# Reordered loads, a longer lead for the gate products and finer routing pieces in a fused attention and mixture-of-experts kernel

## Chip, cores, metric

One core of one Trainium2 chip runs the whole kernel in one launch. All arithmetic is in f32. The metric is the time of one execution on the device in microseconds (us), here the median of 3 runs. Engines are called by the profile's names: PE is TensorE, DVE VectorE, ACT ScalarE, POOL GpSimd, SP SyncE.

## What is computed

The input is q, k, v of 8 batches, 8 heads, 576 positions and 64 channels, and the weights of 8 experts. First comes causal attention in which a position sees itself and the 63 before it; then a mixture of experts on the rows x (4608 rows of 512) that attention gives:

```
scores = where((rel >= 0) & (rel < 64), q @ k.T / sqrt(64), -1e9)
x      = (softmax(scores) @ v), heads side by side          # [8, 576, 512]
logits = x @ w_gate                                          # 8 experts
local  = sigmoid(x @ w_local)
e      = argmax(logits) where s == 0 or local < 0.5, else the e of s - 1
out    = softmax(logits)[e] * (relu(x @ w1[e]) @ w2[e])      # w1 512x1024, w2 1024x512
```

So each row goes to one expert, and whether a row takes its own choice or that of the row before it is settled by a scan along the sequence.

## The kernel before, in words

**Attention** works through 9 superchunks (`sc`) of 512 rows, and in each through 4 pairs of heads (`hp`): 36 units. A unit is `scores` (36 matmuls at L325 into a score bank; ACT's exp at L341; DVE's multiply by a mask at L344) and `values` (32 matmuls at L354; then DVE's reciprocal L359 and products L362 and L364, which make `x`). Scores run two units ahead of values (`LEAD`). Between them PE does helper work, described below.

The orders of PE, ACT and SP are those in which the program is written (`manual_schedule`). POOL and DVE are ordered by a scheduler, which lets DVE run routing work ahead. So where an instruction stands in the text is where it stands in PE's, ACT's and SP's queue, and an early wait there holds up all that is written later.

**Loads.** SP issues them. k and q of a superchunk are four transfers of 512 KB (L198, L199), one pair of heads' halves each, into a ring of four 2 MB slots, which later takes the expert weights too. `va` (L193) holds v with a column of ones behind each head. `vb` holds the same values moved by half a chunk of 128 rows; `shift` fills it by copies, ACT's at L301, L304 and L308, POOL's at L302 and L306 (`shift_first` for superchunk 0, L315 to L317). It is a generator: one or two of its copies are issued per unit, from hp 1 of the superchunk before. `load(sc + 2)` is written at hp 0 and 2 of superchunk sc. `until` (L205) is a transfer of 4 bytes, whose only use is that SP has to wait for what it reads: the loads of superchunk 1 come behind the first mask, those of superchunk 2 behind the reciprocal of unit (0,2).

**Gate.** The logits of x are needed for routing, and they are made in one of two ways. For superchunks 0 to 3, x is transposed by PE (`turn`, L249, copied to SBUF at L252), multiplied with the gate weights (`gates`, L261 to L265; ACT copies the result `gs` at L268), transposed back (`back`, L273), and summed over heads by DVE (`logits`, L279). For superchunks 4 to 8 (from `TURNED` on) the product is taken with v itself, ahead of attention: a transposed v, `vtt`, is loaded (L188), `gates` multiplies it, `back` transposes the result back, and `spread` copies it into 9 further columns of va and vb (ACT L290, L291 and once L293 into vb, DVE L294 into va). `values` then has 74 columns instead of 65, and its weighted sum gives the logits' share of each head along with x. `gates(sc + 1)` is written at hp 2 and `spread(sc + 1)` at hp 3 of superchunk sc.

**PSUM.** Two score banks, and two more tiles of two banks' width, `ps_x`, which values, turn, gates and the routing pieces share. `ps_x` is one pool of two buffers.

**Routing.** `Router.first` routes the first 14 chunks of 128 rows (the first three sequences): argmax, the scan that carries the last fresh choice on (L728 to L758), ranks within an expert, and tables of row numbers (`idx1`, by matmuls at L874). It is a generator too. Each `yield` gives a weight, an estimate of the DVE time since the last one; `step()`, called twice per unit, takes the next piece once the weights, reduced by `HALF` = 0.8 per call, are used up:

```python
    def step():
        nonlocal pause, side
        pause -= HALF
        if side and pause <= 0.0:
            w, trip = next(side, (0.0, None))
            pause = max(pause, -HALF) + w
            if trip is None:
                side = ()
                if ex.jobs:
                    ex.rows(ex.jobs[0], -1)
```

The generator starts at unit (4,2). When it ends, and if the weights of the first expert job have been asked for, the last lines issue the gather of that job's rows (`ex.rows`, POOL L1023, tile `xg`). x of each superchunk is written to DRAM by POOL at L449 (`xs`, 1 MB); gathers read it from there, and both use the same software queue.

**Experts.** `Experts.run` takes six first jobs of 128 rows (numbered from −1), during which `Router.second` routes what remains, and then larger ones of 256 rows. A job gathers its rows, transposes them (PE L1048 into `tp`, copied to `xt` at L1049), multiplies by w1 (`hp`, L1190 and L1099), and by w2 (L1221, L1142), and scatters its rows to the output (POOL L1172). Weights come through the ring (L1035).

Of the kernel before, what the change touches and what calls it, by code (L numbers as in the profile page):

```python
# [60 lines left out]
TURNED = 4  # L61
# [86 lines left out]
def attention(ctx, tc, ring, q, k, v3, v4, vt, xs, lt, ok, wg, wg2, ident, rt, ex):  # L148
# [12 lines left out]

    nc = tc.nc
    cp = ctx.enter_context(tc.tile_pool(name="at_const", bufs=1))
# [4 lines left out]
    ps_x = ctx.enter_context(tc.tile_pool(name="at_ps_x", bufs=2, space=PSUM))  # L168
# [4 lines left out]
    def width(sc):  # L173
        return VX if sc < TURNED else VW

# [3 lines left out]
    def load(sc, parts):  # L179
        t = slice(sc * SC, (sc + 1) * SC)  # L180
        src = v3[t] if sc < TURNED else v4[t.start - TURNED * SC:t.stop - TURNED * SC]
        for part in parts:
            if part == "turned":
                vtt = vts[sc] = kp.tile([P, HP, WIN + SC], F32, name="vtt", bufs=1)

                a = 0 if sc == TURNED else WIN
                at = (sc - TURNED) * SC + a
                nc.sync.dma_start(out=vtt[:, :, a:], in_=vt[:, :, at:at + WIN + SC - a])  # L188
            elif isinstance(part, tuple):
                if sc not in vas:  # L190
                    vas[sc] = space("va", sc)
                h = slice(*part)
                nc.sync.dma_start(out=vas[sc][:, :, h], in_=src[:, h].rearrange("(c p) h x -> p c h x", p=P))  # L193
            else:
                if sc not in kts:
                    both = ring.tile([P, 2, HP, SC], F32, name="w")
                    kts[sc], qts[sc] = both[:, 0], both[:, 1]
                nc.sync.dma_start(out=kts[sc][:, part], in_=k[:, part, t])  # L198
                nc.sync.dma_start(out=qts[sc][:, part], in_=q[:, part, t])  # L199
# [11 lines left out]
    def warm(n):  # L211

        r = ps_x.tile([P, 2, SC], F32, name="xo")
        for _ in range(n):
            nc.tensor.transpose(r[:, 0, :P], ident, ident)

    warm(20)
# [13 lines left out]
    for i in range(2):  # L231
        m = cp.tile([P, KB, 2, WIN], F32, name=f"mask{i}")
        for c in range(2):
            h = slice(c * WIN, (c + 1) * WIN)
            for par in range(2):
                nc.vector.tensor_scalar(m[h, :, par, :], colf[h], rowf[h], None, Alu.is_ge if par == c else Alu.is_lt)
        mid = MID[i]
        other = slice((1 - mid % 2) * WIN, (2 - mid % 2) * WIN)
        nc.vector.memset(m[other, mid // 2, mid % 2, :], 0.0)
        masks.append(m.rearrange("p a b q -> p (a b q)"))  # L240

    allr = cp.tile([P, NSC, HP, 2, 4], F32, name="allr")

    def turn(sc, x, half):

        r = ps_x.tile([P, 2, SC], F32, name="xo")
        for i in range(2):
            for c in range(4):
                nc.tensor.transpose(r[:, i, c * P:(c + 1) * P],  # L249
                                    x[:, c, 2 * half + i].rearrange("p j d -> p (j d)"), ident)  # L250
        o = pp.tile([P, 2, SC], F32, name="p")
        nc.scalar.copy(o, r)  # L252
        vts.setdefault(sc, []).append(o)

    def gates(sc):

        r = ps_x.tile([P, 2, SC], F32, name="xo")
        for hp in range(HP):
            h = slice(hp * GW, (hp + 1) * GW)
            if sc < TURNED:  # L260
                nc.tensor.matmul(r[h, 0, :], lhsT=wg[:, hp, :], rhs=vts[sc][hp // 2][:, hp % 2], start=True, stop=True)  # L261
                continue
            nc.tensor.matmul(r[h, 0, :], lhsT=wg2[:, hp, :], rhs=vts[sc][:, hp, WIN:], start=True, stop=True)
            if sc == TURNED:
                nc.tensor.matmul(r[h, 1, :WIN], lhsT=wg2[:, hp, :], rhs=vts[sc][:, hp, :WIN], start=True, stop=True)  # L265
        n = SC + WIN if sc == TURNED else SC
        gs = wk.tile([P, SC + WIN], F32, name="gs", bufs=1)
        nc.scalar.copy(gs[:, :n], r.rearrange("p i x -> p (i x)")[:, :n])  # L268
        return r, gs
# [11 lines left out]
    def spread(sc, gated):  # L281

        r, gs = gated
        by_head = back(r, gs).rearrange("p (c h g) -> p c h g", c=4, h=H)
        gt = by_head[:, :, :, :E + 1]
        g = slice(VX, VW)
        if sc == TURNED:
            o = r[:WIN, 0, :P]
            nc.tensor.transpose(o, gs[:, SC:], ident)
        nc.scalar.copy(vbs[sc][:WIN, :, :, g], gt[:WIN])  # L290
        nc.scalar.copy(vbs[sc][WIN:, 1:, :, g], gt[WIN:, :3])  # L291
        if sc == TURNED:
            nc.scalar.copy(vbs[sc][WIN:, 0, :, g], o.rearrange("p (h g) -> p h g", h=H)[:, :, :E + 1])  # L293
        nc.vector.tensor_copy(vas[sc][:, :, :, g], gt)  # L294
# [24 lines left out]
    def scores(sc, hp):  # L319
# [24 lines left out]
        nc.vector.tensor_tensor(p, p, m.to_broadcast([P, 2, SC]), op=Alu.mult)  # L344
        return p

    def values(sc, hp, p, x, g):
        va, vb, n = vas[sc], vbs[sc], width(sc)
        xo = ps_x.tile([P, 2, SC], F32, name="xo")
# [11 lines left out]
        if sc >= TURNED:  # L361
            nc.vector.tensor_tensor(g[:, :, hp].rearrange("p c j e -> p j c e"), o[:, :, :, VX:],  # L362
                                    rr.to_broadcast([P, 2, 4, E + 1]), op=Alu.mult)
# [4 lines left out]
    ps = {}  # L368
    for u in units[:LEAD]:
        ps[u] = scores(*u)  # L370
        warm(16)
    shift_first(0)
    until(0, masks[0][:1, :1])
# [16 lines left out]
    def psum():  # L390
        return ps_x.tile([P, 2, SC], F32, name="xo")[:, 0, :]

    for i, (sc, hp) in enumerate(units):
        if hp == 0:
            x, g = wk.tile([P, 4, HP, 2, DH], F32, name="x"), None
            if sc >= TURNED:
# [4 lines left out]
        if hp == 1 and sc + 1 < NSC:  # L401
            moves = shift(sc + 1)
        for _ in range(2):
            next(moves, None) if moves else None
        if hp == HP - 1:
            if sc + 1 < NSC and sc + 1 >= TURNED:
                spread(sc + 1, gated)
            if sc < TURNED:
                turn(sc, x, 0)
                old = x  # L410
        elif 0 < sc <= TURNED:
# [7 lines left out]
        if side is None and 4 * sc >= C1 and hp >= (2 if sc == TURNED else 0):  # L419
# [3 lines left out]
        if i == 0:  # L423
            rt.prepare()
        if i < 2:
            ps[units[i + LEAD]] = scores(*units[i + LEAD])
            if i == 0:
                shift_first(1)
        if hp == 2 and TURNED <= sc + 1 < NSC:
            gated = gates(sc + 1)  # L430
        if sc == 0 and hp == 2:
            until(1, allr[:1, 0, 2, 0, :1])
            load(2, [pairs[0], whole, pairs[1]])
        if 0 < sc < NSC - 2 and hp in (0, 2):
            load(sc + 2, [pairs[1]] if hp else [whole, pairs[0]])
            if hp and sc + 2 >= TURNED:
                load(sc + 2, ["turned"])
# [7 lines left out]
        if hp == HP - 1:  # L445
            if sc >= TURNED:
# [170 lines left out]
class Router:  # L617
# [70 lines left out]
    def gate(self, part, psum):  # L688
# [22 lines left out]
        vec.tensor_tensor(eq, lg, last(mx).to_broadcast(CE), op=Alu.is_equal)  # L711
        vec.tensor_tensor(eq, eq, self.io8m.to_broadcast(CE), op=Alu.mult)
        yield 1.2, False
        own = by_chunk("own")
        vec.tensor_reduce(own, eq, axis=AX.X, op=Alu.min)
        fresh = by_chunk("fresh")
# [4 lines left out]
        yield 1.0, True  # L721
# [9 lines left out]
        vec.tensor_tensor_scan(loc, ts[:, 1, :], ts[:, 0, :], 0.0, Alu.mult, Alu.add)  # L731
        vec.tensor_tensor_scan(thru, ts[:, 1, :], self.zero[:n, :P], 1.0, Alu.mult, Alu.add)
# [17 lines left out]
        vec.scalar_tensor_tensor(ex, thru, cbs, loc, Alu.mult, Alu.add)  # L750
        sm = by_chunk("sm")
# [3 lines left out]
        yield 1.0, True  # L755
# [22 lines left out]
        base = tl("base", P, E * CMAX)[:, :E * n].rearrange("p (e c) -> p e c", e=E)  # L778
        vec.tensor_tensor(base, run, te, op=Alu.subtract)
        yield 1.2, False  # L780
# [4 lines left out]
        if part:  # L785

            vec.tensor_tensor(start, start, self.cnt[0], op=Alu.subtract)
            vec.tensor_tensor(start, start, self.lim1, op=Alu.add)
        vec.tensor_tensor(base, base, last(start).to_broadcast([P, E, n]), op=Alu.subtract)
        vec.tensor_tensor(self.rank[:, cs], pre.rearrange("p (c e) -> p c e", e=E), base.rearrange("p e c -> p c e"),  # L790
                          op=Alu.add)
        vec.tensor_tensor(pa, pa, oh, op=Alu.mult)
        yield 1.2, False
        pt = by_chunk("pt")
        vec.tensor_reduce(pt, pa, axis=AX.X, op=Alu.add)
        vec.tensor_tensor(pt, pt, sm, op=Alu.mult)

# [4 lines left out]
        vec.tensor_tensor(w[:, :, 4], pt, w[:, :, 3], op=Alu.subtract)  # L802

# [6 lines left out]
    def places(self, pl, n):  # L810
# [10 lines left out]
        if n > C1:  # L821
            vec.memset(plc[:CUT, C1:C1 + 1], float(2 * N))
        plc_i = tl("plc_i", P, n, dt=I32)
# [3 lines left out]
        vec.tensor_scalar(plc_i, plc_i, P.bit_length() - 1, None, Alu.arith_shift_right)  # L827
        lo, hi = tl("lo", P, n), tl("hi", P, n)
# [57 lines left out]
    def first(self, psum):  # L886
# [8 lines left out]
        vec.tensor_tensor(foff, fend, nf, op=Alu.subtract)  # L895
        vec.tensor_scalar(fend, fend, float(FIRST), None, Alu.min)
# [4 lines left out]
        yield 1.8, False  # L901
        self.experts_of(tabs["ej1"], FIRST, [(FIRST, fend)])

        CE = [P, C1, E]
# [4 lines left out]
        yield 1.2, False  # L909
        vec.tensor_tensor(pl, pl, mid(foff).to_broadcast(CE), op=Alu.add)  # L910
        vec.tensor_tensor(pl, pl, self.oh[:, :C1], op=Alu.mult)
        lo, hi = self.places(pl, C1)

        vec.tensor_tensor(rank, rank, mid(self.lim1).to_broadcast(CE), op=Alu.subtract)
        yield 2.5, False
        yield from self.table(psum, slice(0, C1), FIRST, lo, hi, tabs["idx1"], tabs["pw1"])

    def second(self, psum):
# [57 lines left out]
        lo, hi = self.places(pl, CV)  # L976
# [20 lines left out]
class Experts:  # L997
# [44 lines left out]
    def turn(self, st, quiet):  # L1042
        nc, n = self.nc, st["rows"]
        st["xt"] = xt = self.wk.tile([P, DK, BIG], F32, name="xt")
# [184 lines left out]
    def space(self, ctx):  # L1229
        tc = self.tc  # L1230
        self.xq = ctx.enter_context(tc.tile_pool(name="ex_xq", bufs=6))
# [111 lines left out]
```

## Time and profile before

| | us |
|---|---|
| median of 3 runs | 668.01 (667.74 to 668.63) |
| span of the profiled execution | 667.3 |
| PE busy | 633.9 (95%) |
| DVE busy | 384.5 (58%) |
| ACT busy | 177.7 (27%) |
| POOL busy | 123.8 (19%) |
| start of the first expert matmul (L1190) | 145.94 |

The busy times say that PE is the engine to watch, but not where it waits. For this the page shows the span in 40 slices, of 16.7 us each, in tenths of busy time:

```profile
PE   8868887889999999999999999999999999999995
PEclk9989999899999999999999999999999999999998
DMA  8699999999887976577559557764865586457540
```

PE is short of full in the first nine slices, which are attention, and full in all that follow. PEclk is the clock that PE was granted; it dips in the third and the eighth slice. The DMA engines are nearly full throughout attention, but for the second slice. In the lists of waits, a line reads: engine, what it was about to work on, what released it; then the sum of the waits, their number, and the longest, in us. In a timeline: start, length, engine, line, operation, what it writes and reads, and in brackets the idle time before it with its releaser. A line of the windows gives from and to, the length, busy times of PE, PEld (its weight loads), DVE, ACT and POOL with their instruction counts, the granted clock, the DMA's share and GB/s.

### The profile page before, as it was taken

To read this page: it belongs to the slowest core of one execution; us is meant where nothing else is said; L and a number is where in the kernel's file an instruction comes from. 1 tells how busy PE (TensorE), PEld (TensorE's weight loads), DVE (VectorE), ACT (ScalarE), POOL (GpSimd) and SP (SyncE) were. 2 spreads that over 40 slices of the span, in tenths; PEclk is the share of its full clock that TensorE was granted. 3 is DMA by queue.
4 is the path that set the end of the run, shared out by engine and by line. 5 is a ranking of instruction groups with operands and counts; after the bars stand their busy time and mean duration, and the time that the engine had idled before them with its cause. 6 is when DMAs were issued, how large, how long until landed. Compare 5 with 4: busy or idle time off the path is not lost. (4 is left out here: it accounts for less than half of the span.)

```text
span 667.3 us, 15133 instructions
## 1 busy us (share of the span) xinstructions
PE 633.9 (95%) x6537; PEld 547.6 (82%) x6537; DVE 384.5 (58%) x693; ACT 177.7 (27%) x274; POOL 123.8 (19%) x128
## 2 busy tenths in 40 slices
PE   8868887889999999999999999999999999999995
PEld 7757766677777789989989998999799979997983
DVE  6645589782961078448638753873566366636410
ACT  2646655431111222303221230312132213211200
POOL 4121112311124111113112211401221121101011
PEclk9989999899999999999999999999999999999998
DMA  8699999999887976577559557764865586457540
GB/s 302 215 383 382 320 371 370 374 353 383 317 301 278 370 281 218 224 281 288 209 174 400 192 217 284 289 237 170 308 227 206 181 316 246 169 182 287 210 153 24
DMA packets 34415, 178.38 MB, mean 267 GB/s; under 512 B 3325, under 2 KB 4355, under 8 KB 27428
## 3 DMA queue, kind: packets, MB, share of 16 engines
q1 hardware_dynamic: 25524, 147.82, 60.6%
q0 software_dynamic: 8816, 29.50, 11.2%
q8 instruction: 54, 0.88, 0.5%
q14 instruction: 21, 0.17, 0.1%
HBM read 158.43 MB, written 19.40 MB: 267 GB/s over the span
## 5 line engine op out<-in xcount | busy, mean ns | idle before, releaser
L1172 POOL DMA_INDIRECT out_dram<-y,idx x36 | 39.9, 1107 | 300.7 <-DVE y L1151 140.8
L1190 PEld LDWEIGHTS hp<-xt,w 128*128 128x128 f32 (+1 forms) x1152 | 88.2, 168 | 4.6 <-issue 3.1
L1190 PE MATMUL hp<-xt,w 128*128 128x128 f32 (+1 forms) x1152 | 89.4, 252 | 1.2 <-ACT xt L1049 1.2
L1099 PE MATMUL hp<-xs,ws 128*128 128x128 f32 x624 | 73.9, 275 | 0.0
L1099 PEld LDWEIGHTS hp<-xs,ws 128*128 128x128 f32 x624 | 71.8, 192 | 0.0
L1142 PE MATMUL hp<-ws,hs 128*128 128x256 f32 x312 | 71.6, 379 | 0.0
L1221 PE MATMUL yp<-w,h 128*128 128x512 f32 x160 | 70.9, 594 | 0.0
L1023 POOL DMA_INDIRECT xg<-xs,idx x40 | 47.2, 1179 | 115.5 <-PE tp L1048 78.8
L1142 PEld LDWEIGHTS hp<-ws,hs 128*128 128x128 f32 x312 | 59.3, 190 | 8.1
L344 DVE TENSOR_TENSOR p<-p,mask 128x1024 f32<-128x1024 f32 x36 | 46.0, 1283 | 23.8 <-ACT p L341 23.6
L1221 PEld LDWEIGHTS yp<-w,h 128*128 128x128 f32 x160 | 29.5, 190 | 32.6 <-issue 31.8
L1110 DVE TENSOR_TENSOR h<-hp,keep 128x512 f32<-128x512 f32 x39 | 27.0, 691 | 49.2 <-PE hp L1099 49.2
L354 PEld LDWEIGHTS xo<-vb,p 128*64 128x64 f32 x576 | 39.0, 139 | 17.4 <-issue 6.1
L354 PE MATMUL xo<-vb,p 128*64 128x74 f32 (+1 forms) x576 | 44.6, 230 | 8.2 <-DVE va L294 2.0
L1099 PEld LDWEIGHTS hp<-xt,w 128*128 128x128 f32 x416 | 49.3, 192 | 3.4 <-issue 2.3
L1099 PE MATMUL hp<-xt,w 128*128 128x128 f32 x416 | 51.0, 276 | 0.0
L341 ACT ACTIVATE p<-sp 128x1024 f32<-128x1024 f32 x36 | 36.8, 1025 | 51.4 <-PE sp L325 46.7
L1151 DVE SCALAR_TENSOR_TENSOR y<-hp,pw,kept 128x256 f32<-128x256 f32 x39 | 18.3, 481 | 55.9 <-issue 33.7
L1142 PE MATMUL hp<-w,h 128*128 128x256 f32 x208 | 49.5, 381 | 0.0
L325 PE MATMUL sp<-w 64*64 64x128 f32 (+1 forms) x1296 | 42.9, 270 | 4.6 <-issue 2.9
L325 PEld LDWEIGHTS sp<-w 64*64 64x64 f32 x1296 | 37.4, 138 | 11.8 <-issue 7.0
L354 PE MATMUL xo<-va,p 128*64 128x74 f32 (+1 forms) x576 | 44.8, 230 | 0.8 <-issue 0.8
(268 smaller groups left out, 905.1 us busy)
## 6 DMA issues: line engine op xcount, KB each, us to landing
w<-in_w_dram SPq DMA_DIRECT2D x54, 2048.0 KB, 8.8
xs<-x POOLq DMA_DIRECT2D x9, 1024.0 KB, 11.5
w<-in_k_dram SPq DMA_DIRECT2D x17, 512.0 KB, 11.3
w<-in_q_dram SPq DMA_DIRECT2D x17, 512.0 KB, 12.1
va<-in_v_dram SPq DMA_DIRECT2D x5, 1184.0 KB, 6.7
vtt<-in_vt_dram SPq DMA_DIRECT2D x4, 1024.0 KB, 7.2
va<-in_v_dram SPq DMA_DIRECT2D x3, 1040.0 KB, 11.8
vtt<-in_vt_dram SPq DMA_DIRECT2D x1, 1152.0 KB
```

The costliest lines, as they stand in the source:

```text
L325: nc.tensor.matmul(sp[c * WIN:(c + 1) * WIN, j, a:b], lhsT=kt[h, hp, block * WIN:(block + 1) * WIN], rhs=qt[h, hp, a:b], start=True, stop= ...
L341: nc.scalar.activation(p, sp, Act.Exp, scale=DH ** -0.5)
L344: nc.vector.tensor_tensor(p, p, m.to_broadcast([P, 2, SC]), op=Alu.mult)
L354: nc.tensor.matmul(xo[par * WIN:(par + 1) * WIN, j, s * VW:s * VW + n], lhsT=p[:, j, b * WIN:(b + 1) * WIN], rhs=w[:, s, 2 * hp + j, :n], ...
L1023: self.nc.gpsimd.indirect_dma_start(out=x, out_offset=None, in_=self.xs[:rows, :], in_offset=bass.IndirectOffsetOnAxis(ap=idx[:, s:s + 1], ...
L1099: nc.tensor.matmul(out[:, m, :], lhsT=a[:, kk, m * P:(m + 1) * P], rhs=b[:, kk, :], start=start and m + kk == 0, stop=stop and (m, kk) == ...
L1110: nc.vector.tensor_tensor(o, x, y, op=add)
L1142: nc.tensor.matmul(out, lhsT=a[:, m, :], rhs=b[:, m, :], start=start and m == 0, stop=stop and m == FK // 2 - 1, skip_group_check=True)
L1151: nc.vector.scalar_tensor_tensor(y[i][:, j * w:(j + 1) * w], x, pw[i], y2, Alu.mult, Alu.add)
L1172: self.nc.gpsimd.indirect_dma_start(out=self.out[:, :], out_offset=bass.IndirectOffsetOnAxis(ap=st["idx"][:, s:s + 1], axis=0), in_=y, in_ ...
L1190: nc.tensor.matmul(hp[a, i, :], lhsT=st["w1"][:, kk, m * P:(m + 1) * P][:, a], rhs=st["xt"][:, kk, :n], start=(kk == 0), stop=(kk == DK - 1))
L1221: nc.tensor.matmul(yp, lhsT=st["h"][:, m, :P], rhs=st["w2"][:, m, :], start=(m == 0), stop=(m == FK - 1))
```

## The change

It has five parts.

1. *Start.* The two runs of idle transposes after the first scores (`warm(16)`) become one (`warm(24)`), the first is shortened from 20 to 12. The second mask and `rt.prepare()` (constants of routing) are built later, after mask multiplies that need DVE first. `until(1, …)` waits for unit (0,0) instead of (0,2), and load(2) is written there. Shift copies begin at hp 3 of superchunk 0, and from then on at hp 0 instead of hp 1.
2. *Gate products.* `GATED = range(4, NSC)` takes the place of `TURNED`. gates(sc + 1) and spread(sc + 1) move one unit earlier where sc is itself gated, so that one more unit lies between the copies and their use. The copy into va goes from DVE to ACT. `vtt` gets a pool of its own (`at_t`).
3. *PSUM in turns.* `ps_x` becomes two pools of one buffer each, and `bank()` takes them strictly in turn.
4. *Routing in pieces.* The generators yield more often, with smaller weights, so that less of DVE's routing work can come in one block. It always starts at hp 2.
5. *Hand-over.* `xt` gets a pool of its own (`ex_xt`), which is to begin in the space that `at_t` leaves.

The rest of the diff prepares v4 and vt for each gated superchunk. Its core:

```diff
+    tp = ctx.enter_context(tc.tile_pool(name="at_t", bufs=1))
-    ps_x = ctx.enter_context(tc.tile_pool(name="at_ps_x", bufs=2, space=PSUM))
+    ps_x = [ctx.enter_context(tc.tile_pool(name=f"at_ps_x{i}", bufs=1, space=PSUM)) for i in range(2)]
+
+    def bank():
+        ps_x.reverse()
+        return ps_x[0].tile([P, 2, SC], F32, name="xo")
...
-    warm(20)
+    warm(12)
...
-        nc.vector.tensor_copy(vas[sc][:, :, :, g], gt)
+        nc.scalar.copy(vas[sc][:, :, :, g], gt)
...
     for u in units[:LEAD]:
         ps[u] = scores(*u)
-        warm(16)
     shift_first(0)
+    with tc.issue_after(masked[-1].ins):
+        build_mask(1)
+    warm(24)
...
-        if hp == 1 and sc + 1 < NSC:
+        if hp == (0 if sc else 3) and sc + 1 < NSC:
             moves = shift(sc + 1)
-        for _ in range(2):
+        for _ in range(2 if sc else 4):
             next(moves, None) if moves else None
+
+        ready = 1 if sc - 1 in GATED else 2
+        if sc + 1 in GATED and hp == ready + 1:
+            spread(sc + 1, gated)
         if hp == HP - 1:
-            if sc + 1 < NSC and sc + 1 >= TURNED:
-                spread(sc + 1, gated)
...
-        if side is None and 4 * sc >= C1 and hp >= (2 if sc == TURNED else 0):
+        if side is None and 4 * sc >= C1 and hp >= 2:
             side = rt.first(psum)
         step()
         values(sc, hp, ps.pop((sc, hp)), x, g)
-        if i == 0:
-            rt.prepare()
         if i < 2:
             ps[units[i + LEAD]] = scores(*units[i + LEAD])
-            if i == 0:
-                shift_first(1)
-        if hp == 2 and TURNED <= sc + 1 < NSC:
+        if i == 0:
+            shift_first(1)
+            until(1, allr[:1, 0, 0, 0, :1])
+            load(2, [pairs[0], whole, pairs[1]])
+        if i == 2 * HP:
+            with tc.issue_after(masked[-1].ins):
+                rt.prepare()
+        if hp == ready and sc + 1 in GATED:
             gated = gates(sc + 1)
-        if sc == 0 and hp == 2:
-            until(1, allr[:1, 0, 2, 0, :1])
-            load(2, [pairs[0], whole, pairs[1]])
...
         vec.tensor_tensor_scan(loc, ts[:, 1, :], ts[:, 0, :], 0.0, Alu.mult, Alu.add)
+        yield 1.6, False
         vec.tensor_tensor_scan(thru, ts[:, 1, :], self.zero[:n, :P], 1.0, Alu.mult, Alu.add)
         yield 1.5, True
...
-        yield 1.0, True
+        yield 0.8, True
...
-        yield 1.2, False
+        yield 0.7, False
...
-        lo, hi = self.places(pl, C1)
+        lo, hi = yield from self.places(pl, C1)
...
-        st["xt"] = xt = self.wk.tile([P, DK, BIG], F32, name="xt")
+        st["xt"] = xt = self.xtp.tile([P, DK, BIG], F32, name="xt")
```

The diff has sixteen more such yields in the routing functions, of 0.4 to 0.8 each.

## The prediction

> **What bounds the kernel now.** I read the windows first, then TensorE's waits, then what stands behind the longest one. The windows give three stages of attention and the expert stage:
>
> ```profile
> 0.00:40.00 40.00, 29.55 (x598) 25.96 (x600) 23.03 (x52) 18.67 (x21) 12.01 (x28) 0.99 0.81 283
> 40.00:85.00 45.00, 41.11 (x925) 33.70 (x927) 26.32 (x42) 27.64 (x34) 8.71 (x9) 0.97 0.99 352
> 85.00:145.94 60.94, 48.94 (x1193) 40.21 (x1193) 54.11 (x155) 29.29 (x40) 14.29 (x13) 0.97 0.99 366
> 145.94:667.30 521.36, 514.26 (x3828) 447.73 (x3828) 281.06 (x445) 102.07 (x181) 88.84 (x78) 1.00 0.66 247
> ```
>
> The first busy figure is TensorE's. From 145.94 it has no gap until the last results leave, and the change hardly touches that stage. Before 145.94 its single gaps add up to 26.3 us; that is all there is to win. The largest, from the waits:
>
> ```profile
> PE xo L273 <- ACT gs L268: 6.0, 4, 5.0
> PE sp L325 <- issue: 2.9, 3, 1.4
> PE xo L215 <- POOL ident masks.py:199: 2.6, 1, 2.6
> PE xo L354 <- DVE va L294: 2.0, 1, 2.0
> ...
> PE xo L354 <- ACT p L252: 1.5, 1, 1.5
> PE hp L1190 <- ACT xt L1049: 1.2, 1, 1.2
> ...
> PE xo L354 <- DVE t L876: 1.0, 1, 1.0
> ```
>
> The longest (last column) is 5.0 us at L273, released by ScalarE's `gs` copy. ScalarE's timeline tells why that copy was late:
>
> ```profile
> 37.12 1.05 ACT L304 COPY vb<-va 64x1040 f32<-64x1040 f32 x1 [4.68 <-DMA va<-in_v_dram]
> 38.20 0.59 ACT L268 COPY gs<-xo 128x512 f32<-128x512 f32 x1
> ```
>
> SyncE's own timeline, where the DMA loads are issued, tells why va(2) was late:
>
> ```profile
> 24.48 0.62 SPq L205 DMA_DIRECT2D late<-allr  x1
> 25.15 0.38 SPq L198 DMA_DIRECT2D w<-in_k_dram  x1
> ```
>
> And two windows show what the DMA did meanwhile:
>
> ```profile
> 20.00:22.50 2.50, 0.85 (x30) 0.71 (x28) 0.52 (x1) 2.48 (x3) 1.91 (x2) 1.00 0.24 83
> 22.50:25.00 2.50, 1.99 (x34) 1.61 (x28) 2.47 (x4) 1.79 (x3) 0.00 (x0) 1.00 0.00 0
> ```
>
> The gs copy stands behind L304 in ScalarE's order, L304 waits for va(2), and the loads of superchunk 2 were held until 24.48 by `until`, with the DMA idle (last two columns: share and GB/s) from about 20.5 to 26.5. GpSimd's timeline shows the end of attention:
>
> ```profile
> 129.13 1.05 POOL L1023 DMA_INDIRECT xg<-xs,idx  x1 [3.56 <-DVE allr L359]
> 130.48 1.01 POOL L1023 DMA_INDIRECT xg<-xs,idx  x1 [0.30 <-issue]
> 138.11 0.80 POOL L449 DMA_DIRECT2D xs<-x  x1 [6.62 <-DVE x L364]
> ```
>
> The gather of the first expert job is issued 9 us ahead of the write xs(7), and lands at 139.18, before its transposes at 142.43 (L1048).
>
> **What the Trainium skill says.** "TensorE: Matmul & The Clock Gate", What's actually happening: after an idle window of about 3.4 us the clock falls to half until a busy window has passed. The trace agrees: after the 5.03 us gap the granted clock is about 0.5 from 38.88 to 42.29, 3.41 us; after gaps of 1.65 and 1.98 us none follows. "DMA: Bandwidth & Descriptors", Queues, rings and completion order: a DMA engine takes turns between queues packet by packet. The trace agrees: xs(6), issued at 124.81 beside weight loads (16 KB packets of 0.62 us against 4 KB of 0.16), landed at 138.54, after 13.7 us; the gather queued behind it on the same queue landed 0.6 us later; xs(7) without weights moved in 3.5 us (139.5 to 143.0).
>
> **Part 1, start and early loads: gain 5.9 us.** Routing's preparation no longer stands in front of the first mask multiply on VectorE (exp done 9.81, multiply started 12.67), so values(0,0) moves from 14.04 to about 12.2. `until` now waits for the reciprocal of unit (0,0), so load(2) follows load(1) at 14 to 16 instead of 25.15, and the DMA runs on through the 6 idle us. Before, va(2) landed 10.6 us after the DMA took up again (37.09 − 26.5), with xs(0)'s 1 MB among it, 2.7 us at the 370 to 400 GB/s of the full windows; in the changed order that write stands behind the shift copies, so 20.5 + 7.9: va(2) lands at about 28.3 (27.5 to 29.7) instead of 37.09. The shift of superchunk 2 now stands one unit earlier on ScalarE, ahead of the turn copy at (1,0), so gates(0) waits for va(2) plus two copies and the turn (1.05 + 1.02), 30.4. Queued behind that wait: gs, L273, scores(2,1). Chaining the durations (scores 1.12, values 1.15, turn 1.09, gates 1.05, back 0.66, exp 1.02) and the bank waits of superchunk 1, scores(2,1) ends at 37.2; before it is at 43.12. If the wait still costs a half-clock window, 4.2 us remain; with va(2) at 27.5, 7.
>
> **Part 2, PSUM in turns: loss 1.5, gain 0.6.** The pool of two buffers gave whichever bank was free; `bank()` alternates strictly. values(sc,2) then takes the bank that `back` filled for logits, and must wait for its reduce on VectorE: the reduce (L279) is 0.31, with the hand-overs to it and back about 0.5, and nothing is beside it on TensorE. Superchunks 2, 3 and 4: 3 × 0.5 = 1.5. Against it, values(3,3) waits for the last spread copy rather than for the turn copy (1.5 in the list), worth 0.6. The spread on ScalarE costs 0.45 more there (L294's duration), hidden since it now stands a unit or more before values of that superchunk.
>
> **Part 3, routing in pieces: loss 0.7.** More yields of 0.4 to 1.6 put PE's routing pieces later; the table ends after (7,3) rather than at (7,1). Removed: the waits 1.98 (L294) and 1.00 (L876), the 0.5 and 0.7 at ts, thru and ex in part. Added, since a routing piece on TensorE takes its bank in turn and VectorE runs routing ahead in its own order: values(5,0) 0.2, tp 0.45, values(5,1) and (5,2) 1.65 each (its bank's last reader behind a 1.31 us scan and a 1.23 us multiply), values(6,0) 2.05 behind `rank`. Following the chain with the durations above, from the start of values(4,2) to that of (6,1) come 27.6 us against 26.2 (84.88 to 111.10); from there to the end of values(7,3), where two of the old waits are gone and up to 2 us of new ones lie partly beside other work, 24.9 against 25.6. Net −0.7, good to ±2.
>
> **Part 4, hand-over: loss 3.5, and 1.7 of clock.** Call V the end of values(7,3) (136.7 before). `first` now ends behind it, and the end of it issues the gather. So GpSimd has xs(7) first, then the gather, on one queue. In order: x(7,3) is done at V + 2.0; xs(7) moves from V + 3.5 to V + 7.0 (1.4 us to its first packet and 3.5 of packets, as measured); idx is ready at V + 3.05, but the gather's 256 KB stand behind xs(7). The loads of job −2 start packets at about V + 6.3 (142.5 less 136.7, and the table's half us), so each of the gather's four 4 KB packets per DMA engine takes turns with one of 16 KB: 4 × (0.62 + 0.16) = 3.1, plus 0.7 to landing: V + 10.8. TensorE has after V the table (0.5), scores and values of superchunk 8, 6.8 us, and then stands at tp for 4.0. From tp to the first expert matmul the change is quicker: xt has a pool of its own and waits for x(8,2), not x(8,3): 1.9 instead of 3.5. V to hp: 6.8 + 4.0 + 1.9 = 12.7 against 9.24 before: 3.5 lost. An idle stretch of 4 us brings a half-clock window as at 38.88: 3.4 × 0.5 = 1.7. From below: if weights start later, the gather lands at V + 8.5, the stall is 1.7 and only 1.2 is lost; from above, as starved as gather(−3) of before (8.4 us from issue to landing, in all), V + 14 and 6.7 lost.
>
> **Part 5, expert stage: loss 0.5.** One flag transpose (L141) now stands where it waits for a copy of about 0.5; routing's second part ends one job sooner, with 6.9 us of VectorE beside 7.5 us of TensorE, hidden. The rest has the same matmuls (514.26 us).
>
> **Sum:** 5.9 + 0.6 − 1.5 − 0.7 − 3.5 − 1.7 − 0.5 = −1.4, so 668.0 + 1.4 = 669.4 us.
>
> **Rivals.**
> A. Faster. The gather lands in time and the clock holds: part 4 costs 1.2 instead of 5.2, and the sum is +2.6: 665.4; with routing at even, 664.7. For it: w(−2) is bound by its own issue and may start later; 4.0 is hardly over a clock window. Against: xs(7) must move first, whatever the weights do.
> B. No difference. Gather at V + 9.5, no clock loss: part 4 costs 2.2 and the routing pieces 2 more than counted; 668.4. For it: every part ends in waits of half a us that I took from order, not from measurement.
> C. Clearly slower. Gather at V + 14 (6.7 and 1.7), early gain 4.2 since the wait at gates(0) also costs a clock window: 4.2 + 0.6 − 1.5 − 0.7 − 8.4 − 0.5 = −6.3: 674.3. For it: xs(6)'s 13.7 us beside weights. Against: xs(7) begins before the loads of −2.
>
> **How the numbers follow.** Forecast 0.36, A 0.32, B 0.15, C 0.17. The forecast lies at the edge of "same", so some of it goes there: faster 0.35, same 0.20, slower 0.45. Range: A's lower end with part 1 at 5.9 and routing at +0.3 gives 664.0; C's upper end is cut to 674.0. What is left out is about 0.1 on each side.
>
> **What would show it.** Part 1: load(2) issued by 16, no DMA idle at 20 to 26, scores(2,1) ended near 37, a wait of 1 to 3 us at gates(0). Part 2: values(sc,2) waiting for the logits reduce, 0.5 each. Part 3: waits at values(5,1), (5,2), (6,0); no wait for L294. Part 4: GpSimd's order xs(7), gather; a wait of tp or of its weight load for xg of about 4 us, then a clock near 0.5. No such wait, or the gather issued before xs(7), makes the forecast wrong and A right; a start of the expert stage later than 150 makes C right.

## The result

The changed kernel takes 678.18 us, median of 6 runs (676.72 to 680.49), against 668.11 (667.05 to 671.12) for the kernel before in the same comparison: a ratio of 1.0149, 95% interval 1.0122 to 1.0175. It is slower by about 10 us. The forecast was 669.4 with a range to 674.0: the side was right, the size was not.

The windows of the changed kernel's profile (span 675.8), over the same stages as before; the first busy figure is TensorE's, the last three columns are granted clock, DMA share and GB/s:

```profile
0.00:40.00 40.00, 31.01 (x660) 27.45 (x662) 24.38 (x39) 19.95 (x23) 13.82 (x27) 0.96 0.96 338
40.00:85.00 45.00, 38.85 (x881) 31.15 (x884) 27.42 (x59) 27.62 (x35) 9.06 (x10) 1.00 0.96 337
85.00:152.71 67.71, 49.16 (x1161) 40.57 (x1153) 52.08 (x144) 30.19 (x42) 13.74 (x13) 0.96 0.90 325
152.71:675.80 523.09, 515.41 (x3830) 449.33 (x3828) 281.88 (x448) 102.17 (x181) 89.38 (x78) 1.00 0.66 244
```

The DMA is now full from the start (0.96 for 0.81), and TensorE has done 660 matmuls by 40 us, for 598 before. But the third stage ends at 152.71 instead of 145.94. From there to the end it takes 523.09 for 521.36, of which a wait of 0.62 for routing's `vk`, one of 0.50 at the flag transpose and the rest of a half-clock window account for most.

TensorE's waits up to 160 us in the changed kernel (sum, number, longest); a wait called issue is one in which TensorE waited for nothing that the profile shows:

```profile
PE xo L363 <- issue: 4.3, 4, 1.9
PE xo L258 <- issue: 3.6, 2, 3.1
PE tp L1073 <- DMA xg<-xs,idx: 3.5, 1, 3.5
PE sp L334 <- issue: 3.4, 4, 1.3
...
PE xo L363 <- DVE sh_i L827: 3.3, 1, 3.3
PE xo L363 <- ACT va L303: 2.6, 2, 1.7
...
PE xo L363 <- DVE lt L288: 1.9, 4, 0.5
PE xo L270 <- ACT p L261: 1.8, 3, 0.8
```

The wait for `gs` (5.0 before) and the one for VectorE's `va` copy are gone. New are the wait of the first expert transposes for `xg`, a wait of values for a bank that VectorE's routing holds (`sh_i`), waits for ScalarE's spread copy (L303), and four of 0.5 for the logits reduce (L288). Waits called issue are 12.7 us for 5.7.

Where the front gained, in ScalarE's timeline of the changed kernel; the shift copy L313, which before waited 4.68 us for va(2), starts at once:

```profile
30.32 1.05 ACT L313 COPY vb<-va 64x1040 f32<-64x1040 f32 x1
31.40 1.01 ACT L261 COPY p<-xo 128x1024 f32<-128x1024 f32 x1
...
34.01 0.59 ACT L277 COPY gs<-xo 128x512 f32<-128x512 f32 x1
```

And the end of attention, in GpSimd's timeline of the changed kernel:

```profile
140.09 0.75 POOL L463 DMA_DIRECT2D xs<-x  x1 [10.33 <-DVE pw L904]
141.51 1.05 POOL L1048 DMA_INDIRECT xg<-xs,idx  x1 [0.67 <-DVE idx L903]
142.87 1.01 POOL L1048 DMA_INDIRECT xg<-xs,idx  x1 [0.30 <-issue]
```

The gather of the first expert job is issued at 141.51, as soon as its index is there, and behind xs(7), as forecast. Before it was issued at 129.13. From 141.5 to 144.2 the queue that both use (q0) moves the packets of xs(7) (packets, MB, share of the DMA engines):

```profile
q0 software_dynamic: 236, 0.95, 97.1%
```

The gather's packets come after that, among those of the weight loads, which begin at 145.1. The transposes of its rows could have begun at 146.35, and began at 149.86; a half-clock window follows (granted 0.55 from 149.9 to 153.3).

Starts of units on TensorE in us, read from the traces (values of superchunk, head pair; tp are the first expert transposes, hp the first expert matmuls). The names of the experiments are explained below.

```
          before   after   e1      e8      e9      e4      e10
(2,0)      47.23   43.77   41.97   43.69   42.02   42.48   44.07
(4,0)      78.42   74.78   72.24   74.41   73.54   72.70   74.03
(7,3)     134.47  136.37  132.52  130.45  129.63  132.66  132.25
tp        142.43  149.86  140.50  138.50  137.78  147.22  141.76
hp        145.94  152.71  142.48  140.69  141.30  150.40  143.90
```

Up to (4,0) the changed kernel is 3.6 us ahead; between (4,0) and (7,3) it loses 5.5; from (7,3) to hp it takes 16.3 for 11.5. Each column is one execution, and it need not be a typical one: that of e10 is the fastest of its four (669.0 us, median 673.59), that of e1 the fastest of its twelve (666.5, median 669.43).

### The profile page after: what moved, and what is told of

Its sections match the earlier page's. It is cut to its first block, busy times and chain, and to the rows that moved or that the text cites. A ratio compares the mean times of both kernels' runs of the same rounds, so it can differ in the third digit from the quotient of the medians.

```text
span 675.8 us, 15102 instructions
## 1 busy us (share of the span) xinstructions
PE 634.4 (94%) x6521; PEld 548.5 (81%) x6521; DVE 385.8 (57%) x688; ACT 179.9 (27%) x279; POOL 126.0 (19%) x128
## 5 line engine op out<-in xcount | busy, mean ns | idle before, releaser
L363 PE MATMUL xo<-vb,p 128*64 128x74 f32 (+1 forms) x576 | 46.5, 235 | 14.1 <-issue 4.0
L363 PEld LDWEIGHTS xo<-vb,p 128*64 128x64 f32 x576 | 40.7, 143 | 22.8 <-issue 14.4
L363 PE MATMUL xo<-va,p 128*64 128x74 f32 (+1 forms) x576 | 46.7, 235 | 0.3 <-issue 0.3
```

The source lines that it names most:

```text
L363: nc.tensor.matmul(xo[par * WIN:(par + 1) * WIN, j, s * VW:s * VW + n], lhsT=p[:, j, b * WIN:(b + 1) * WIN], rhs=w[:, s, 2 * hp + j, :n], ...
```

## Experiments

First four runs, each undoing or doing one thing. Medians of the kernel before in the comparisons: 667.5 to 668.1.

**e1_routing_back.** The routing generators (class Router) as before, all else as changed; the first of its lines:

```diff
-        yield 0.6, False
         vec.tensor_tensor(eq, eq, self.io8m.to_broadcast(CE), op=Alu.mult)
+        yield 1.2, False
         own = by_chunk("own")
         vec.tensor_reduce(own, eq, axis=AX.X, op=Alu.min)
-        yield 0.7, False
...
```

> The changed kernel with the routing generators' yields of before (all of part 3 undone, parts 1, 2, 4 and 5 kept). Its routing ends two units earlier, so the gathers of jobs -1 and -2 stand ahead of xs(7) on GpSimd. Theory P (the pieces: the later end of routing, and DVE's routing work between TensorE's units, carry the loss): the wait for xg is gone, values(5,0) to values(6,0) lose their waits, time 667 to 670. Theory B (strict turns of the PSUM banks carry it): the wait for xg is gone (3.5), but the waits of values for DVE's routing work stay or grow, 673 to 676. Theory F (instruction fetches carry it, 12.7 us of waits called issue against 5.7 before): 674 or more, with issue still over 10.

Measured: 669.43 us, ratio to before 1.0023 (1.0006 to 1.0041). The wait for xg is gone. The finer pieces cost 8.8 us of the changed kernel's time (678.18 − 669.43). Theory P holds in its time and in the wait for xg; B's 673 and F's 674 are missed. One sign of P did not come: values(5,2) still waits 1.68 us, for ScalarE's spread copy, as in the changed kernel.

**e2_psum_free.** One pool of two PSUM buffers:

```diff
-    ps_x = [ctx.enter_context(tc.tile_pool(name=f"at_ps_x{i}", bufs=1, space=PSUM)) for i in range(2)]
+    ps_x = ctx.enter_context(tc.tile_pool(name="at_ps_x", bufs=2, space=PSUM))
     def bank():
-        ps_x.reverse()
-        return ps_x[0].tile([P, 2, SC], F32, name="xo")
+        return ps_x.tile([P, 2, SC], F32, name="xo")
```

> The changed kernel with one PSUM pool of two buffers, as before, instead of two banks in turn (part 2 undone alone). Theory B: the waits of values for lt L288 (1.9), va L303 (2.6), crow L755 (1.5) and sh_i L827 (3.3) go, 9 us in sum, of which some 2 to 3 come back as other waits: 670 to 673. Theory P: the pieces stand where they stood, 676 to 679. Theory F: issue stays over 10, 676 or more.

Measured: 677.34 us, 1.0109 (1.0074 to 1.0144). B's 670 to 673 is missed, P's 676 to 679 is met. TensorE could have begun the first expert job at 140.67 in this trace, and waits 7.9 us for xg there.

**e3_load_only.** The kernel before with the early load alone:

```diff
-        if sc == 0 and hp == 2:
-            until(1, allr[:1, 0, 2, 0, :1])
+        if sc == 0 and hp == 0:
+            until(1, allr[:1, 0, 0, 0, :1])
             load(2, [pairs[0], whole, pairs[1]])
```

> The kernel before with the loads of superchunk 2 behind the reciprocal of (0,0), not (0,2), and nothing else. Theory L (the early load is worth what the trace of the changed kernel shows up to unit (4,0), 3.6 us, and the 5.03 us wait at L273 with its half-clock window goes): 663.5 to 665.5. Theory F (removed waits come back as waits for instructions, since the DMA is now full where the third fetch falls): 666.5 to 668.5, issue up by 2 to 3.

Measured: 665.84 us, 0.9959 (0.9945 to 0.9973), between the two ranges. These are its waits (TensorE's, first 160 us):

```profile
PE xo L354 <- issue: 4.9, 6, 1.5
PE xo L215 <- POOL ident masks.py:199: 2.6, 1, 2.6
PE sp L325 <- issue: 2.4, 2, 1.4
...
PE xo L273 <- ACT gs L268: 1.0, 3, 0.4
```

The wait for gs fell from 6.0 to 1.0, which is theory L. Issue rose from 5.7 to 7.3; that is less than two traces of one program differ by (see the last section), so that theory F's exchange of waits took place is not shown.

**e4_gather_first.** The write xs(7) behind the gather of job −1 (`ex.gathered`, the last gather that `ex.rows` issued):

```diff
-            nc.gpsimd.dma_start(out=xs[sc * SC:(sc + 1) * SC, :].rearrange("(c p) d -> p c d", p=P),
-                                in_=x.rearrange("p c h j d -> p c (h j d)"))
+            with tc.issue_after(ex.gathered.ins) if sc == NSC - 2 else ExitStack():
+                nc.gpsimd.dma_start(out=xs[sc * SC:(sc + 1) * SC, :].rearrange("(c p) d -> p c d", p=P),
+                                    in_=x.rearrange("p c h j d -> p c (h j d)"))
```

> The changed kernel with the write xs(7) held behind the gather of job -1 on GpSimd, and nothing else: same routing, same banks. Theory T (the gather is late because 1 MB stands ahead of it on its queue): the wait of tp for xg falls from 3.5 to under 0.5, the first expert matmul starts about 3.5 us earlier relative to the end of values(7,3), 674 to 675. Rival (the gather is late by its index, or by the weight loads beside it): the wait is 2.5 or more, 677 to 679.

Measured: 677.11 us, 1.015 (1.0105 to 1.0196); no different from the changed kernel. GpSimd's timeline of e4_gather_first, then the wait:

```profile
137.58 1.77 POOL L1049 DMA_INDIRECT xg<-xs,idx  x1 [12.89 <-DVE idx L904]
139.35 0.79 POOL L464 DMA_DIRECT2D xs<-x  x1
```

```profile
PE tp L1074 <- DMA xg<-xs,idx: 5.8, 1, 5.8
```

With nothing ahead of it on its queue the gather still took from 137.58 to 147.08, 9.5 us. Between 137.6 and 142.7 the DMA moved none of its packets, but 78 of the weight loads of job −2, which here begin 1.3 us after the gather was issued (the only other packet is one of instructions):

```profile
q1 hardware_dynamic: 78, 1.28, 77.6%
q8 instruction: 1, 0.02, 1.1%
```

Theory T falls: taking xs(7) out of the gather's way does not make it early. In the changed kernel xs(7) did stand ahead of it; without xs(7), the weight loads hold it up as long.

The next four runs ask whether the late end of routing is the cause, and what the rest of the change costs without it.

**e5_pieces_alone.** The kernel before with the changed kernel's class Router and nothing else; one of the nineteen yields that are new or in a new place:

```diff
         vec.tensor_tensor_scan(loc, ts[:, 1, :], ts[:, 0, :], 0.0, Alu.mult, Alu.add)
+        yield 1.6, False
         vec.tensor_tensor_scan(thru, ts[:, 1, :], self.zero[:n, :P], 1.0, Alu.mult, Alu.add)
```

> The kernel before with the finer yields of the change and nothing else of it. Theory E (the later end of routing is the cause: the index of the first gather comes some 3 us before its transposes need the rows, and a gather beside weight loads takes 8 to 11 us to land): 675 to 677, a wait of tp for xg of 4 to 8 us, and a half-clock window behind it. Rival I (the pieces hurt only together with PSUM in turns or the longer lead): 668 to 670.

Measured: 680.01 us, 1.0205 (1.0143 to 1.0267). The two signs of theory E came, its time is 3 us above its range; rival I is out. The waits of e5_pieces_alone from 80 to 165 us, and the clock in the windows behind the wait (0.51 and 1.00, third column from the right):

```profile
PE tp L1059 <- DMA xg<-xs,idx: 7.2, 1, 7.2
PE xo L354 <- DVE va L294: 2.6, 2, 2.1
PE xo L354 <- DVE x L364: 2.3, 2, 1.4
```

```profile
151.80:155.20 3.40, 3.26 (x36) 2.74 (x36) 0.06 (x1) 0.01 (x1) 0.95 (x1) 0.51 1.00 426
155.20:158.60 3.40, 2.28 (x20) 2.31 (x21) 3.37 (x12) 0.93 (x2) 0.80 (x1) 1.00 0.48 188
```

One line tells it: 7.2 us of waiting for xg, then 3.4 us at half speed. The pieces need no help from the rest of the change to do their harm.

**e6_dense_pieces.** The changed kernel, with all its pieces, but taken as fast as their weights allow:

```diff
-HALF = 0.8
+HALF = 0.85
...
         pause -= HALF
-        if side and pause <= 0.0:
+        pause = max(pause, -HALF)
+        while side and pause <= 0.0:
             w, trip = next(side, (0.0, None))
-            pause = max(pause, -HALF) + w
+            pause += w
```

> The changed kernel, all pieces as they are, but step() takes as many pieces as their weights allow (a while in place of an if) and HALF is 0.85, so that routing ends at (7,1) as before. Theory E: no wait for xg, 668 to 671. Rival (the pieces' own waits between the units, about 5 us of dependency waits in superchunks 5 and 6, are the loss): 674 or more.

Measured: 668.99 us, 1.0021 (1.0008 to 1.0034). The gather is issued early again, in GpSimd's timeline of e6_dense_pieces:

```profile
129.03 1.05 POOL L1049 DMA_INDIRECT xg<-xs,idx  x1 [3.85 <-DVE allr L368]
130.38 1.01 POOL L1049 DMA_INDIRECT xg<-xs,idx  x1 [0.30 <-issue]
136.74 0.80 POOL L464 DMA_DIRECT2D xs<-x  x1 [5.35 <-DVE x L373]
```

So it isn't the number of the pieces by itself, nor their length. `step()` takes at most one piece in half a unit; before there were 15 to take and now there are 26, and so routing ended at (7,3) instead of (7,1), whatever the weights said. Taking several at once gives back 9.2 us with every piece in place.

**e7_psum_routing_back** is e1 with e2's edit added; **e8_gates_routing_back** is e1 with

```diff
-        ready = 1 if sc - 1 in GATED else 2
+        ready = 2
...
-        nc.scalar.copy(vas[sc][:, :, :, g], gt)
+        nc.vector.tensor_copy(vas[sc][:, :, :, g], gt)
```

> e1_routing_back with one PSUM pool of two buffers as before. Theory B2 (of the 3.6 us by which e1_routing_back is behind the kernel before with the early load alone, the strict turns carry most: lt L288, va L303 and x L373 waits of about 6 us in its trace): 665.5 to 667.5. Rival: 669 to 670.

> e1_routing_back with gate products and spread at the units of before and the va copy on DVE. Theory G (the longer lead and ScalarE's copies carry most of the 3.6 us): 665.5 to 667.5. Rival: 669 to 671, with the wait for va by DVE of 2 us back.

Measured: e7 667.21 us, 0.9993 (0.997 to 1.0015); e8 666.24, 0.9983 (0.9964 to 1.0002). Both lie in the range of their theory: each part costs something.

**e9_start_and_handover** is e1 with both edits, so that only the start with its early loads and the hand-over are left of the change.

> The changed kernel with parts 2, 3 and 4 undone (gate products, PSUM and routing as before), so only the start with the early loads and the hand-over remain. From the runs so far: the early load alone gives 2.2 us, undoing the turns 2.2 and undoing the longer lead 3.2 of e1_routing_back's 669.4. If these add: 663.5 to 665.5, faster than both kernels. Rival (they overlap: both only exchange the same waits): 666 to 667.5.

Measured: 664.06 us (661.64 to 665.78), 0.9934 (0.9914 to 0.9954), faster than both kernels. The four kernels e1, e7, e8 and e9 make a square: without the longer lead, strict turns cost 666.24 − 664.06 = 2.2; with it, 669.43 − 667.21 = 2.2. Without turns, the lead costs 667.21 − 664.06 = 3.2; with them, 669.43 − 666.24 = 3.2. The executions of each kernel spread over 4 to 7 us, and the median of the kernel before moved by 0.5 between the comparisons. Taken against it, the same four figures are 2.7, 1.7, 3.7 and 2.7. So each of the two costs something and they add within 1 to 2 us; that the medians agree to a tenth is chance. e8 takes back two things at once, the place of the gate products and the engine of the copy into va, and which of the two costs was not separated.

Where the lead's cost sits, the starts of units tell in part. From (4,0) to (7,3) the traces without the lead and with routing as before take 56.1 (before), 55.3 (e3), 56.0 (e8) and 56.1 (e9), those with the lead 60.3 (e1) and 58.7 (e7). With the lead, gates(7) stands right behind values(6,1), and in e1 the waits come close together there: 0.60 of issue and 2.00 for x before values(6,1), 1.39 of issue at L272. Two windows at that place, of e1_routing_back first, then of e8_gates_routing_back, then of e9_start_and_handover:

```profile
108.80:112.20 3.40, 2.24 (x32) 2.05 (x32) 3.40 (x8) 0.81 (x2) 0.75 (x1) 0.61 1.05 392
112.20:115.60 3.40, 2.11 (x14) 0.47 (x18) 3.37 (x10) 0.12 (x1) 0.00 (x0) 0.50 1.03 381
```

```profile
108.80:112.20 3.40, 3.40 (x106) 3.18 (x102) 3.40 (x9) 2.58 (x3) 0.00 (x0) 1.00 1.03 368
112.20:115.60 3.40, 1.70 (x31) 0.73 (x30) 3.40 (x8) 0.44 (x2) 0.00 (x0) 1.00 1.03 410
```

```profile
105.40:108.80 3.40, 2.58 (x62) 2.49 (x66) 3.29 (x12) 1.76 (x2) 2.19 (x2) 0.82 1.00 385
108.80:112.20 3.40, 3.40 (x82) 3.20 (x74) 3.40 (x9) 1.71 (x2) 0.00 (x0) 0.68 1.01 316
```

In e1 the clock is at about half for most of 6.8 us, in which TensorE does 46 matmuls for 137 in e8, and e7 has the same picture (0.53 and 0.50). But it is not the clock that sets the two pairs apart: e9, without the lead, also has a half-clock window here, from 107.58 to 110.99, and an earlier one from 90.51 to 93.93. So the lead's cost lies between (4,0) and (7,3), and which wait in that stretch carries it stays open.

**e10_weights_behind** is e4 with the weight loads of job −2 held until the gather has landed:

```diff
-    late = cp.tile([1, 2], F32, name="late")
+    late = cp.tile([1, 3], F32, name="late")
...
+            until(2, ex.jobs[0]["x"][0][:1, :1])
             ex.jobs.append(ex.weights({}, -2))
```

> e4_gather_first (gather of job -1 ahead of xs(7)) with the weight loads of job -2 held on SyncE until that gather has landed. Theory W (the gather takes 9.5 us because of the weight packets beside it): it lands within 5 us of its issue, the wait of tp for xg falls from 5.8 to under 2, 673 to 675. Rival (the latency of a gather is its own): landing stays at 8 us or more, the wait at 4 or more, 677 or more.

Measured: 673.59 us, 1.0095 (1.0072 to 1.0119). The time from a gather's issue to its landing (min/median/max of the gathers between 120 and 160 us), e4_gather_first first, e10_weights_behind second:

```profile
DMA to landing us min/median/max: 8.6/9.5/16.1
```

```profile
DMA to landing us min/median/max: 3.6/7.0/15.2
```

The 3.6 is the gather of job −1 (137.18 to 140.82), the same gather that took 9.5 in e4. TensorE doesn't wait for it. All three signs of theory W came. So the weight loads beside it, not its own latency, make a gather slow. The weights of job −2 then come later; in this trace no wait of TensorE is for them. The median is still more than 4 us above e1 and e6, and the trace, of the fastest execution, does not show why.

**e11_few_loads** asks about the waits called issue:

```diff
                 if sc not in kts:
+                if sc > 4:
+                    kts[sc], qts[sc] = kts[4], qts[4]
+                    continue
```

> The kernel before without the k and q loads of superchunks 5 to 8 (their scores are computed from superchunk 4's k and q, so this part of the result is left out). If TensorE's waits called issue, 5.2 us between 60 and 137 in the kernel before, come from its instruction fetches queueing behind these loads, they fall below 1 us there; if the fetch is slow by itself, they stay at 3 or more.

Measured: 671.84 us, 1.0056 (1.0038 to 1.0073). Issue between 60 and 137 us is 0.54 + 2.29 + 0.36 = 3.2 for 5.2, with the DMA's share down from about 1.0 to 0.6 between 75 and 120. It did not go away. By the letter of the expectation 3.2 speaks for a fetch that is slow by itself, but traces of one program differ by far more than this (see the last section), and these are two executions, 3.8 us slower than the kernel before for reasons that were not looked into. The question stays open.

## Why the prediction was right and wrong

The forecast can be set against the runs group by group, since e9, e8, e1 and the changed kernel are four steps of one path (gain positive, us):

| group | forecast | measured | from |
|---|---|---|---|
| start and early loads | +5.9 | +4.0 | before 668.05, e9 664.06 |
| turns and hand-over | −0.9 + 1.6 | −2.2 | e8 − e9 |
| longer lead, spread by ScalarE | 0 | −3.2 | e1 − e8 |
| routing in pieces, with the wait at tp, its clock, and the expert stage | −8.0 | −8.8 | after − e1 |
| sum | −1.4 | −10.2 | |

**The step that failed** is a term set to zero. The longer lead was costed at nothing, with the sentence that ScalarE's copies are hidden since they stand a unit or more ahead. It cost 3.2 us by the medians, the largest mis-sized term of the sum. What I weighed was the copy's 0.45 us; what I did not ask was where the moved gates product would stand, and behind which wait. The runs show the size and that it lies between units (4,0) and (7,3); whether the place of the gates product or the copies on ScalarE carry it was not separated. Turns with the hand-over, forecast as a gain of 0.7, are off by nearly as much, 2.9.

**Part 1.** Right in kind: load(2) left at 14.68, the DMA had no idle, L313 did not wait. Over-sized by 1.9. The early load alone gave 2.2 (e3). In the changed kernel's trace scores(2,1) ended at 38.9 instead of 37.2. There a wait of 3.1 us at the first turn (L258) was not in the chain; nothing in the profile releases it, and a half-clock window follows it (23.94 to 27.36). Of the traces with the same front, those of e6 and e10 have such a wait (3.1 and 2.8) and those of e1 and e4 do not, so it belongs to the execution and not to the change.

**Part 2, turns.** The waits for the logits reduce came as forecast, 0.47 four times. What the forecast missed is that these were not all: the bank in turn also ties values to ScalarE's spread copy. In e1, which has turns, values waits 4.0 us for that copy; in e7, which lacks them, 0.9.

**The hand-over** from tp to hp took 2.0 in e1 and 2.2 in e8, as forecast (1.9). In e9 it took 3.5 as before, and in e7 3.7, although xt has its own pool there: TensorE waits for x again (1.4). The gain comes only with the turns, and the forecast did not see that. Nor did it see that most of it goes again: e1 and e8 wait 1.05 for routing's `vk` in the expert stage, e7 and e9 do not.

**Part 3 and 4.** The sum of the pieces' cost was nearly right, 8.0 for 8.8, and in part by luck. In part 3 two waits of the right size came, values(5,1) 1.5 and values(5,2) 1.7 for 1.65 each, but the second is for ScalarE's spread copy and is there in e1 too, without the pieces. The third, forecast as 2.05 behind `rank` before values(6,0), came as 3.3 behind `sh_i`. In part 4, routing's late end, the order xs(7) before the gather, and a stall at tp with a half-clock window all came: 3.5 in the trace for a forecast of 4.0. Also as forecast, xs(7) and then the weights kept the gather waiting. What was wrong is the belief that the order decides it: with xs(7) out of the way the stall remains (e4). The gather's index comes 3.5 to 4.8 us before its rows are needed (e2, e4, e5 and the changed kernel), while beside weight loads it takes 8 to 11 us to land (8.3 in the changed kernel to the end of the wait, 9.5 in e4, 10.7 in e5, 11.3 in e2; without them 3.6, in e10). The stalls of 3.5 to 7.9 are the difference.

The rows were counted as four packets per DMA engine with one weight packet between, 3.1 us. In e4's trace the first of them moved only 5.2 us after the issue, and they took 3.9 more. The trace of before had this too: the first packet of xs(6) came 4.1 us after its issue beside weight loads, that of xs(7) 1.4 without. The taking of turns by packet, which the forecast reckoned with, does not cover this first delay.

The stall also hides what the turns cost: in e2 tp waits 7.9, 4.4 more than in the changed kernel's trace. That is likely why undoing the turns, worth about 2 once routing ends early, brought nothing clear there (677.34 for 678.18).

**Rivals.** C, the slower one, named the starved gather, with an end 14 us after values(7,3); it was given 0.17. The forecast's own sign for C, an expert stage that starts later than 150, came (152.71). It was nearest, at 674.3, and still short.

**The range** ended at 674.0, below C's own figure. It took in the unknown of the gather and of the clock, but not that a move costed at nothing could cost 3 us: terms set to zero had no width. Its lower end has a slip: A with routing at +0.3 gives 664.4, not 664.0; nothing hangs on it.

## What to carry to other kernels

When a generator's pieces are fed into a schedule one per slot, the number of pieces sets when it ends, not their weights. Count the slots, and see what waits for the end; a fine grain that helps at each slot can push the last result past the point where its transfer was hidden. A small gather that starts beside large loads should be priced by a gather of the same trace that also ran beside them (8.4 us was in the trace of before, and stood only in the rival), not by its bytes. And give a range to each term that is set to zero.

## What the runs showed of the hardware

The changed kernel and e4 give TensorE the same instructions in the same order; only one write on GpSimd stands elsewhere. In the trace of one, TensorE's waits called issue sum up to 12.7 us ahead of the expert stage, in that of the other to 2.3. In the other traces they lie between 3.1 and 10. In most of them a 16 KB packet on the instruction queue ends shortly before TensorE goes on, 1.0 to 1.6 us before, in the kernel before too (62.15 and 63.60, 128.43 and 129.94). Not all of them can be matched so, and e11 did not remove them, so their cause is not settled. But it means that differences of a few us between two single traces of such kernels can't be read as effects of an edit; the timed runs of the square e1, e7, e8 and e9 were needed for that.

The "TensorE: Matmul & The Clock Gate" page of the Trainium skill (What's actually happening) has the clock halve after an idle window of about 3.4 us. The prediction's reading, that the trace agrees, left out a second half-clock window of the kernel before, from 117.38 to 120.80, with no wait longer than 1.11 ahead of it. It came after waits of 0.93 and 1.11 within 3.4 us; in e1 the clock was at half from 109.55, after waits of 0.60 and 2.00 within 3.4 us; after the single wait of 1.98 at 106.89 in the kernel before it did not fall. These are the 3.41 us ahead of the two falls, and those with the single wait (first busy figure: TensorE's), of the kernel before, of e1, and of the kernel before:

```profile
113.97:117.38 3.41, 1.37 (x28) 0.78 (x24) 3.41 (x8) 1.81 (x3) 0.00 (x0) 1.00 1.03 368
```

```profile
106.14:109.55 3.41, 1.12 (x26) 0.74 (x18) 3.41 (x7) 2.89 (x4) 0.00 (x0) 1.00 1.03 402
```

```profile
107.14:110.55 3.41, 1.68 (x51) 1.60 (x55) 3.34 (x9) 0.86 (x1) 2.79 (x3) 1.00 1.04 395
```

TensorE is busy for 40% and 33% of the time ahead of the falls, for 49% where none followed. Within a trace the falls lie whole multiples of 3.41 us apart (38.88 and 117.38 are 23 such steps). Counted on that raster over all 13 traces up to the first expert job, 25 of the 26 falls from full clock come after a step in which TensorE was busy for 45% or less (the other, at 90.51 in e9, after 54%), and every step at full clock that no fall followed had 47% or more. So a step that is mostly idle, and not only one without any work, was enough in these traces.
